# The shifted copies of the VectorE score groups are made on GpSimd, with 16 VectorE tiles per block

## The chip, the cores and the metric

The kernel runs on one core of a Trainium2 chip. The metric is the device time of one execution in microseconds (us). Three runs of the kernel before took 776.45, 778.93 and 774.36 us; the median is 776.45.

The core has five engines that run side by side, each in the order of its own list of instructions: PE (TensorE, matrix products), ACT (ScalarE, exponentials), DVE (VectorE), POOL (GpSimd) and SP (SyncE, which here issues nearly all DMAs). They wait for each other through semaphores.

## The reference

Two attentions share one input and are mixed by a gate. S is 2048, D is 512, there are 32 heads of 16.

```python
# A: linear attention with softmax features
phi_q = concat([softmax(pq), softmax(-pq)]);  phi_k = concat([softmax(pk), softmax(-pk)])
kv = einsum("bhsf,bhsd->bhfd", phi_k, v);  z = einsum("bhsf->bhf", phi_k)
o_A = einsum("bhqf,bhfd->bhqd", phi_q, kv) / (einsum("bhqf,bhf->bhq", phi_q, z)[..., None] + 1e-6)
# B: full attention
p = softmax(einsum("bhqd,bhkd->bhqk", q, k) * 16 ** -0.5)
o_B = einsum("bhqk,bhkd->bhqd", p, v)
g = sigmoid((x * gate_w).sum(-1))
out = g * (o_A @ A_wo) + (1 - g) * (o_B @ B_wo)
```

Nearly all the work lies in B: 32 heads of 2048 x 2048 scores, each of which needs an exponential.

## The kernel before

**Blocks and tiles.** B is cut into 32 blocks. A block is four heads and 512 queries; it has 16 tiles of 128 keys for each head, so 64 tiles of 128 x 512 scores, and 2048 tiles in all. The scores of a tile come from PE (`qk_mm`, line 782), land in PSUM and are made into exponentials in bf16. PE then multiplies them by the values (`pv_mm`, line 883) and adds them up in PSUM (psO); a column of ones in the values gives the sum of each softmax.

**Two ways to an exponential.** Most tiles go through ACT: `add_exp` (line 859) takes three tiles and two tiles by turns in one instruction (line 862), from one half of the six banks of psS. Those instructions are the slots by which the rest of the order is counted. The list DN (line 31) says how many tiles of each block take the other way, through DVE. There a tile is made in an integer: DVE reads the scores, adds a constant, clamps at zero and writes an int16 (line 840), whose bits, read as bf16, are a rough exponential. To make it better, the kernel uses three such values for each score, the number itself (t) and the number plus 35 (s) and plus 83 (m) (STEPS, line 28), and PE adds up all three: three matmuls a tile (`add_pvd`, line 886) where a tile of ACT needs one.

**Groups.** DVE's tiles are handled in groups of up to four (`add_group`, line 827). The scores of each tile go to a free bank (psM or the last bank of psS) by a matmul of their own; four evictions (line 840) fill a buffer t of 128 x 2048. Then two additions (line 853) write the buffers s and m. They are DVE instructions on int16 in SBUF. The buffers are taken in turn from rings of three or four (t), three (s) and three or two (m), mostly memory that other steps don't need at that time, which is why one line shows many tile names (Tx, Ty, vA, WAT, WoA and so on). A group can reuse a buffer once PE has read the old one. A field `pool` of each group is set from the list PN (line 56) at line 710; nothing in the kernel before reads it.

**Other work.** A's features are made 128 rows at a time in `phi` (line 1098): PE, two exponentials on ACT (line 1105), a sum of pairs on POOL (line 1110), a row sum and reciprocal on DVE (1112, 1114) and two products on POOL (line 1118). 16 such steps make phiK, one per 13 slots from slot 40, and 16 make phiQ, one per 14 slots from slot 270. For each pair of blocks, POOL also multiplies the result by its reciprocal sums (T2, line 983). The projections, A's second half and the output fill PE and DVE between the tiles. SP moves q, phiQ, the sums and the output.

**Order.** Nothing runs in the order in which the program names it. Each operation is given to a planner (`Plan`) with an engine, an estimated duration and a priority; `layout` (line 149) plays the execution through with these estimates and writes one fixed list for each engine. `emit` then puts a semaphore wait wherever an operation needs another engine's result. A group's operations carry priorities some 22 slots (D_AHEAD) ahead of the slot where its tiles are due. Operations marked `lock` on DVE (the additions, line 853, and one product per late block, line 998) and on POOL are laid apart in time: a locked POOL operation also waits for the last locked DVE operation ahead of it (lines 311 to 314). PE gets matmuls by zero (`zero_mm`, line 871) where the plan would leave it idle; they add nothing to the result.

Of the kernel before, what the change touches and what calls it, by code (L numbers as in the profile page):

```python
# [11 lines left out]
ALU = mybir.AluOpType  # L12
# [13 lines left out]
QSCALE = 0.25 * LOG2E * 2.0 ** 7  # L26
EXPB = 127.0 * 2.0 ** 7 - 252.7
STEPS = (35, 83)
ESCALE = math.log(2.0) / 2.0 ** 7

DN = (0, 10, 14, 16, 14, 16, 14, 16, 14, 16, 14, 16, 14, 16, 14, 16, 14, 16, 14, 16, 14, 16, 14, 16, 14, 16, 14, 16, 14, 16, 14, 12)
G_EARLY = 13
W_AT = 18.0
D_FIRST = 12
# [18 lines left out]
TURN_PAD = 4.0  # L53
G_DEEP = 6
K_AT, K_PACE, Q_AT, Q_PACE = 45.0, 13.0, 275.0, 13.5
PN = (1, 2, 1, 2, 1, 2, 1, 2, 1, 2, 1, 2, 1, 2, 1, 2, 1, 2, 1, 2, 1, 2, 1, 2, 1, 2, 1, 2, 1, 2, 1, 2)
D_AHEAD = 22.0
CONT = -60.0
EPAIRS = 5
# [326 lines left out]
def bass_gated_mix__linear_kernel_hedgehog__mha_block__prompt_kernel(  # L386
    nc: bass.Bass,
    A_x: bass.AP,
    A_wqkv: bass.AP,
    A_w_phi: bass.AP,  # L390
    A_wo: bass.AP,
    B_x: bass.AP,
    B_wqkv: bass.AP,
    B_wo: bass.AP,
    gate_w: bass.AP,
    out: bass.AP,
):
    with contextlib.ExitStack() as ctx:
        _build(ctx, nc, A_x, A_wqkv, A_w_phi, A_wo, B_wqkv, B_wo, gate_w, out)


def _build(ctx, nc, A_x, A_wqkv, A_w_phi, A_wo, B_wqkv, B_wo, gate_w, out):
# [71 lines left out]
    P = Plan()  # L474
# [20 lines left out]
    for rr in range(8):  # L495
# [4 lines left out]
                  name="woa", lat=5.0),  # L500
              dma("sp", 2.2, lambda e: e.dma_start(WoB[:], B_wo.rearrange("(t p) c -> p t c", p=128)), ["WoB"],
                  name="wob", lat=5.0)]
# [3 lines left out]
    def warm_fn(e):  # L506
        ins = None
        for _ in range(6):
# [5 lines left out]
    pool = lambda dur, prio, fn, reads=(), writes=(), name="": P.add("pool", dur, prio, fn, reads=reads,  # L514
                                                                    writes=writes, name=name)
# [3 lines left out]
         writes=["ident"], name="ident")  # L519
# [9 lines left out]
          writes=["pmask0"], name="pm0")  # L529
    P.add("dve", 0.1, -9, lambda e: e.tensor_scalar(pmask[:, 1:2], pmask[:, 0:1], -QSCALE, QSCALE, op0=ALU.mult,  # L530
                                                    op1=ALU.add), reads=["pmask0"], writes=["pmask1"], name="pm1")
    P.add("dve", 0.1, -9, lambda e: e.tensor_single_scalar(pmask[:, 0:1], pmask[:, 0:1], QSCALE, ALU.mult),
          reads=["pmask1"], writes=["pmask", "pmask0"], name="pm2")
# [6 lines left out]
    for t in range(KT):  # L540
# [12 lines left out]
          writes=["mtmp1"], name="mk0")  # L553
    P.add("dve", 0.12, 30, lambda e: e.tensor_single_scalar(mask64[:], m1, 16, ALU.is_lt), reads=["mtmp1"],
          writes=["mask64"], name="mk1")
    pool(0.3, -2, lambda e: e.tensor_copy(mask4[:], mask64[:].rearrange("p (j c) -> p j c", c=16)[:, :, 0]),
         reads=["mask64"], writes=["mask4"])
# [3 lines left out]
    def fill(prio, mms, reads, banks=None, name="", chunk=1, dur=MM, after=(), cols=NQ):  # L561

        f = Fill(MISC if banks is None else banks)
        prev = None
        for i in range(0, len(mms), chunk):
            part = mms[i:i + chunk]

            def fn(e, part=part):
                ins = None
                for m in part:  # L570
                    ins = m(e, f.ap())
                return ins
            op = P.add("pe", dur * len(part), prio if prev is None else CONT, fn, reads=reads if prev is None else (),
                       after=after if prev is None else [prev], name=f"{name}.{i}")
            op.full, op.fill = cols / 2400.0 * len(part), True
            if prev is None:
                op.acq = f
            prev = op
        for k in reads:
            P.readers.setdefault(k, []).append(prev)  # L580
        return f, prev

    def drain(f, mm, eng, dur, prio, fn, reads=(), writes=(), name="", last=True, after=()):
        op = P.add(eng, dur, min(prio, -20.0) if eng == "dve" else prio, lambda e: fn(e, f.ap()), reads=reads, writes=writes, after=[mm] + list(after),
                   name=name)
        if last:
            op.rel = f
        return op
# [109 lines left out]
    slots = []  # L698
    assert all(n % 2 == 0 for n in DN)
    dcount = [[0] * 4 for _ in range(NB)]  # L700
    dtiles, groups, turn = [], [], 0
    for b in range(NB):
        for k in range(DN[b]):
            i = (k + turn) % 4
            dcount[b][i] += 1
            dtiles.append(dict(t=(b, i, NT - dcount[b][i]), k=k))
        turn += DN[b]
        mine = dtiles[len(dtiles) - DN[b]:]
        for n in range(0, DN[b], 4):
            groups.append(dict(ts=mine[n:n + 4], left=len(mine[n:n + 4]), pool=n // 4 < PN[b] and len(mine[n:n + 4]) == 4))  # L710
    cur, rot = 0, 0

    def next_tile():
# [49 lines left out]
    def opening(name):  # L763
        if name in opened:
            return []
        opened.add(name)
        return list(bufs[name][1])

    def quarter(ap, q):
        if len(ap.shape) == 3:  # L770
            return ap[:, q // 2, 512 * (q % 2):512 * (q % 2) + 512]
        return ap[:, 512 * q:512 * q + 512]
# [7 lines left out]
    def qk_mm(e, t, bank):  # L780
        b, i, kt = t
        return e.matmul(bank, lhsT=kT_B[32 * i:32 * i + 32, b // 8 % 2, 128 * kt:128 * (kt + 1)],  # L782
                        rhs=qz[32 * i:32 * i + 32, b // 2 % 4, b % 2, :], start=True, stop=True,
                        tile_position=(32 * i, 0))
# [30 lines left out]
    def make_groups(n):  # L815
        for g in groups[made[0]:n]:
            if any(k in holder and holder[k]["left"] for k in (g["t"], g["s"], g["m"])):
                break
            holder[g["t"]] = holder[g["s"]] = holder[g["m"]] = g
            add_group(g)  # L820
            made[0] += 1

    def d_prio(d):
        b = d["t"][0]
        return first_slot[b] + d["k"] * 20.0 / DN[b] - D_AHEAD

    def add_group(g):
        t, s, m = (bufs[g[k]][0] for k in "tsm")
        ft, ops, tb = opening(g["t"]), [], t
        before = list(dq_ops)  # L830
        dq_ops.clear()
        for q, d in enumerate(g["ts"]):
            b, i, kt = d["t"]
            f, mm = fill(DQ_PRIO + DQ_K * d_prio(d), [lambda e, ap, t=d["t"]: qk_mm(e, t, ap)],
                         [kkey(b // 8, kt), ("q", b // 2 % 4, b % 2)], name=f"dq{b}.{kt}.{i}", dur=0.25,
                         after=[exp_ops[D_FIRST]] + ft + P.writer.get((g["t"], q), []) +
                         P.readers.get((g["t"], q), []) + before, cols=NQ)
            dq_ops.append(mm)
            mm.kind, mm.heads = "dq", [i]
            ops.append(drain(f, mm, "dve", 0.70, d_prio(d), lambda e, ap, q=q: e.tensor_scalar(  # L840
                quarter(tb, q).bitcast(I16), ap, EXPB, 0.0, op0=ALU.add, op1=ALU.max),
                writes=[(g["t"], q)], after=ft, name=f"D1.{b}.{kt}.{i}"))

        def add(dur, fn, reads, writes, name, after=()):
            ops.append(P.add("dve", dur, d_prio(g["ts"][0]) - 5.0, fn, reads=reads, writes=writes, after=after,
                             name=f"{name}.{b}.{kt}"))
            ops[-1].lock = True
        size = len(g["ts"])
        part = lambda ap: ap[:, 0:512 * size].bitcast(I16)
        t, s, m = part(t), part(s), part(m)  # L850
        tk = [(g["t"], k) for k in range(size)]
        for key, dst, step in (("s", s, STEPS[0]), ("m", m, STEPS[1])):
            add(0.72 if size == 4 else 0.45, lambda e, dst=dst, step=step: e.tensor_single_scalar(dst, t, step, ALU.add),  # L853
                tk, [g[key]], "D2" if key == "s" else "D3", opening(g[key]))
        if g is groups[-1]:
            last_d1.extend(ops[:size])
        phase_ops[g["ph"]].extend(ops)

    def add_exp(j):
        n = len(slots[j])  # L860
        base = 3 * (j % 2)
        op = P.add("act", 0.051 + 0.4267 * n, 0.0, lambda e: e.activation(  # L862
            Ebuf[:, j // 2 % EPAIRS, 1536 * (j % 2):1536 * (j % 2) + 512 * n], psS[:, 512 * base:512 * (base + n)], ACTF.Exp, scale=ESCALE),
            reads=[("S", j % 2)], writes=[("E", j % ERING)], name=f"exp{j}")
# [336 lines left out]
    for i in range(4):  # L1201
        mms = [lambda e, ap, i=i, t=t: e.transpose(ap.bitcast(BF16)[:, 128 * t:128 * (t + 1)],
                                                   xs[:, i, 128 * t:128 * (t + 1)], ident[:]) for t in range(KT)]
        f, mm = fill(-1.0, mms, [("xs", i), "ident"], FIRST, name=f"X{i}", chunk=4, dur=0.08, cols=128)
        x_mms.append(mm)
        dst = xT[:, :, 128 * i:128 * (i + 1)]
# [142 lines left out]
```

## Time and profile before

| | before |
|---|---|
| runs | 776.45, 778.93, 774.36 us (median 776.45) |
| span of the profiled execution, first to last instruction | 774.6 us |
| its own time | the profile gives the span alone |
| mean granted clock of TensorE | 0.991 |
| busy: PE, ACT, DVE, POOL | 718.3, 757.2, 585.0, 137.0 us |
| exponentials of three tiles, of two tiles (line 862) | 318, 319 |
| evictions of DVE tiles (line 840) | 456, median 0.68 us |
| additions (line 853) | 212 of 2048 elements, 32 of 1024; 160.9 us busy |
| POOL instructions | 32 at line 1110, 64 at line 1118, 15 at line 983, 30 at the start |

How to read it: busy time is the time in which an engine has at least one instruction under way. ACT's records overlap, since an instruction starts before the one ahead of it has ended; so the distance from start to start, not the length of a record, is what one instruction costs. A row of the groups gives line, engine and operation, output and input, partitions x elements and type, the count, then busy us and mean ns of one, then the idle time ahead of the group and what ended it. A row of the waits reads "who waited <- for whom: us in total, times, longest". "PEld" is PE's weight load, with which each matmul starts.

### The profile page before, as it was taken

The numbers are of one execution on the slowest core, as the hardware profiler recorded it, in microseconds if no ns is written. First come the engines' busy times: TensorE is split into PE (matmuls) and PEld (weight loads), VectorE is DVE, ScalarE is ACT, GpSimd is POOL, SyncE is SP. The second block draws the span as 40 slices with busy tenths as digits, with TensorE's granted clock in tenths as the row PEclk, the third lists the DMA queues.
The fourth block names the chain that finished last, engine by engine and source line by source line (L and its number), as shares of the span: only waits on it lengthen the run. The fifth ranks groups of instructions, "written<-read, shape, count | busy, mean of one in ns | idle before, by whom it ended". The sixth has DMA issues, their size and how long they took to land.

```text
span 774.6 us, 17058 instructions
## 1 busy us (share of the span) xinstructions
PE 718.3 (93%) x7135; PEld 223.1 (29%) x7194; DVE 585.0 (76%) x1023; ACT 757.2 (98%) x708; POOL 137.0 (18%) x141
## 2 busy tenths in 40 slices
PE   8999989998999999989999999998999998999999
PEld 4332222332322222332322222222232222222222
DVE  3667877777778888567898897987887778787842
ACT  6999999999999999999999999999999999999996
POOL 6001032112322131200313121231311200000000
PEclk9999999999999999998999999999999999999999
DMA  6600000000000100201002221322311221020101
GB/s 128 146 9 16 20 14 21 10 23 9 10 17 9 24 8 8 72 8 23 23 27 60 55 71 44 82 68 51 83 53 38 73 53 37 22 64 3 46 13 48
DMA packets 67933, 30.72 MB, mean 40 GB/s; under 512 B 53208, under 2 KB 62808, under 8 KB 67856
## 3 DMA queue, kind: packets, MB, share of 16 engines
q1 hardware_dynamic: 66368, 28.95, 14.9%
q8 instruction: 56, 0.92, 0.5%
q10 hardware_dynamic: 1104, 0.66, 0.3%
q0 software_dynamic: 384, 0.02, 0.1%
q14 instruction: 21, 0.17, 0.1%
HBM read 7.87 MB, written 8.88 MB: 22 GB/s over the span
## 4 chain that ended last, share of the span: by engine, by line
ACT 84%; PE 11%; DVE 4%; SPq 1%; DMA 1%; issue 1%
ACT E_t L862 80%; ACT EA_t L1105 3%; PE psS L782 3%; PE psO L883 3%; PE psM L591 1%; PE psS L591 1%; DVE Tx_t L840 1%; DVE WAT_t L840 1%; PE psO L873 1%; DMA xT_t<-in_A_x_dram 1%; SPq L486 0%; DVE vA_t L853 0%; PE psS L651 0%; DVE vA_t L840 0%; DVE Ty_t L853 0%
## 5 line engine op out<-in xcount | busy, mean ns | idle before, releaser
L862 ACT ACTIVATE E_t<-psS 128x1536 bf16<-128x1536 f32 x637 | 731.9, 1419 | 5.4 <-PE psS L782 3.7
L782 PE MATMUL psS<-qz_t,kTB_t 32*128 32x512 bf16 x1815 | 277.0, 387 | 41.9 <-ACT E_t L862 34.1
L782 PEld LDWEIGHTS psS<-qz_t,kTB_t 32*128 32x128 bf16 x1815 | 69.2, 91 | 277.8 <-ACT E_t L862 242.3
L883 PE MATMUL psO<-E_t,vaug_t 128*32 128x512 bf16 (+1 forms) x1592 | 141.1, 389 | 0.7 <-DVE vaug_t L647 0.5
L840 DVE TENSOR_SCALAR Tx_t<-psS 128x512 int16<-128x512 f32 x121 | 82.4, 681 | 27.2 <-PE psS L782 24.6
L840 DVE TENSOR_SCALAR Tx_t<-psM 128x512 int16<-128x512 f32 x127 | 86.8, 683 | 19.4 <-PE psM L782 17.7
L873 PE MATMUL psO<-xT_t,zero_t 128*32 128x512 bf16 x1076 | 93.8, 387 | 0.0
L1110 POOL TENSOR_TENSOR half_t<-EA_t 128x512 f32<-128x512 bf16 x32 | 37.0, 1155 | 314.0 <-ACT EA_t L1105 273.4
L782 PE MATMUL psM<-qz_t,kTB_t 32*128 32x512 bf16 x233 | 90.1, 387 | 0.7 <-DVE Tx_t L840 0.2
L883 PE MATMUL psO<-vA_t,vaug_t 128*32 128x512 bf16 (+1 forms) x430 | 58.7, 387 | 0.0
L883 PE MATMUL psO<-Ty_t,vaug_t 128*32 128x512 bf16 (+1 forms) x308 | 50.4, 390 | 0.0
L1118 POOL TENSOR_TENSOR phiQ_t<-EA_t,stat_t 128x512 bf16<-128x512 bf16 x32 | 34.2, 1070 | 72.2 <-DVE stat_t L1114 61.7
L983 POOL TENSOR_TENSOR oT_t<-Tf_t,Rb_t 128x512 bf16<-128x512 f32 x15 | 19.1, 1272 | 157.4 <-DVE Ty_t L853 91.1
L883 PEld LDWEIGHTS psO<-E_t,vaug_t 128*32 128x32 bf16 (+1 forms) x1592 | 29.0, 95 | 59.8 <-issue 57.1
L1118 POOL TENSOR_TENSOR phiK_t<-EA_t,stat_t 128x512 bf16<-128x512 bf16 x32 | 33.8, 1058 | 60.4 <-DVE stat_t L1114 31.3
L883 PE MATMUL psO<-Tx_t,vaug_t 128*32 128x512 bf16 (+1 forms) x248 | 38.5, 398 | 0.0
L873 PEld LDWEIGHTS psO<-xT_t,zero_t 128*32 128x32 bf16 x1076 | 23.3, 94 | 41.3 <-issue 36.2
L853 DVE TENSOR_SCALAR vA_t<-Tx_t 128x2048 int16<-128x2048 int16 x50 | 34.1, 686 | 0.1
L853 DVE TENSOR_SCALAR Ty_t<-Tx_t 128x2048 int16<-128x2048 int16 x42 | 29.8, 709 | 0.4
L840 DVE TENSOR_SCALAR WAT_t<-psM 128x512 int16<-128x512 f32 x37 | 25.2, 682 | 5.9 <-PE psM L782 3.8
L840 DVE TENSOR_SCALAR WAT_t<-psS 128x512 int16<-128x512 f32 x39 | 26.6, 682 | 2.2 <-PE psS L782 1.9
L782 PEld LDWEIGHTS psM<-qz_t,kTB_t 32*128 32x128 bf16 x233 | 21.1, 91 | 23.1 <-issue 6.7
(188 smaller groups left out, 768.1 us busy)
## 6 DMA issues: line engine op xcount, KB each, us to landing
dpq<-phiQ_t SPq DMA_DIRECT2D x16, 256.0 KB, 2.1
Rb_t<-lr SPq DMA_DIRECT2D x120, 32.0 KB, 1.8
dpo<-oA_t SPq DMA_DIRECT2D x16, 128.0 KB, 1.8
qz_t<-qz_t SPq DMA_DIRECT2D x120, 16.0 KB, 1.8
Tf_t<-Tf_t SPq DMA_DIRECT2D x60, 32.0 KB, 2.0
out_dram<-WvA_t SPq DMA_DIRECT2D x14, 128.0 KB, 1.7
WB_t<-in_B_wqkv_dram SPq DMA_DIRECT2D x3, 384.0 KB, 4.4
WvA_t<-in_A_wqkv_dram SPq DMA_DIRECT2D x1, 512.0 KB, 4.0
```

Source lines behind the costliest of these rows:

```text
L591: return [lambda e, ap, i=i: e.matmul(ap, lhsT=lhs[i], rhs=rhs[i], start=(i == 0), stop=(i == len(lhs) - 1)) for i in range(len(lhs))]
L782: return e.matmul(bank, lhsT=kT_B[32 * i:32 * i + 32, b // 8 % 2, 128 * kt:128 * (kt + 1)], rhs=qz[32 * i:32 * i + 32, b // 2 % 4, b % 2, ...
L840: ops.append(drain(f, mm, "dve", 0.70, d_prio(d), lambda e, ap, q=q: e.tensor_scalar(quarter(tb, q).bitcast(I16), ap, EXPB, 0.0, op0=ALU.a ...
L853: add(0.72 if size == 4 else 0.45, lambda e, dst=dst, step=step: e.tensor_single_scalar(dst, t, step, ALU.add), tk, [g[key]], "D2" if key ...
L862: op = P.add("act", 0.051 + 0.4267 * n, 0.0, lambda e: e.activation(Ebuf[:, j // 2 % EPAIRS, 1536 * (j % 2):1536 * (j % 2) + 512 * n], psS ...
L873: ins = e.matmul((psO if bank is None else bank)[32 * i:32 * i + 32, :], lhsT=zero[:], rhs=xT[:, 0, 0:NQ], start=bank is not None, stop=ba ...
L883: return e.matmul(psO[32 * i:32 * i + w, :], lhsT=vaug[:, kt, o:o + w], rhs=rhs, start=start, stop=stop, tile_position=(0, 32 * i), skip_g ...
L983: P.add("pool", 1.1, -40, lambda e: e.tensor_tensor(oT[:, r, qc, :], Tf[:, 0, :], Rb[:], ALU.mult), reads=[("Tf", 0), "Rb"], writes=[("oT" ...
L1105: ins = e.activation(EA[:, b, :].rearrange("p (g s c) -> p s g c", s=2, c=64)[:, sgn, :, :], ap.rearrange("p (g c) -> p g c", c=64), ACTF. ...
L1110: P.add("pool", 1.15, prio, lambda e: e.tensor_tensor(half[:], e3[:, :, 0:8], e3[:, :, 8:16], ALU.add), reads=[("EA", b)], writes=["half"] ...
L1118: parts.append(P.add("pool", 1.0, prio, lambda e, n=n: e.tensor_tensor(dst[:, 512 * n:512 * n + 512].rearrange("p (g f) -> p g f", f=DH), ...
```

## The change

The two additions of every group go from DVE to POOL. There each is one `tensor_scalar` with two operations, times 1.0 and plus 35 or 83. The planner is told 0.2 us plus 512 x tiles / 1200 us for it (1.9 us for four tiles), it has the same priority as before, and it is marked `lock`. PN is 4 for all blocks, and the condition that a group has four tiles is gone, so all groups take this way. With no additions on DVE, its only locked operation left is the product of the last blocks. DN becomes 16 for all blocks but the first three and the last, where 14 and 16 took turns: DVE tiles go from 456 to 484, tiles of ACT from 1592 to 1564.

```diff
+G_FIX = 0.2
-DN = (0, 10, 14, 16, 14, 16, 14, 16, 14, 16, 14, 16, 14, 16, 14, 16, 14, 16, 14, 16, 14, 16, 14, 16, 14, 16, 14, 16, 14, 16, 14, 12)
+DN = (0, 10, 14) + (16,) * 28 + (12,)
-PN = (1, 2, 1, 2, 1, 2, 1, 2, 1, 2, 1, 2, 1, 2, 1, 2, 1, 2, 1, 2, 1, 2, 1, 2, 1, 2, 1, 2, 1, 2, 1, 2)
+PN = (4,) * 32
-            groups.append(dict(ts=mine[n:n + 4], left=len(mine[n:n + 4]), pool=n // 4 < PN[b] and len(mine[n:n + 4]) == 4))
+            groups.append(dict(ts=mine[n:n + 4], left=len(mine[n:n + 4]), pool=n // 4 < PN[b]))
         for key, dst, step in (("s", s, STEPS[0]), ("m", m, STEPS[1])):
+            if g["pool"]:
+                ops.append(P.add("pool", G_FIX + 512 * size / 1200.0, d_prio(g["ts"][0]) - 5.0, lambda e, dst=dst, step=step: e.tensor_scalar(
+                    dst, t, 1.0, float(step), op0=ALU.mult, op1=ALU.add), reads=tk, writes=[g[key]],
+                    after=opening(g[key]), name=f"G{key}.{b}.{kt}"))
+                ops[-1].lock = True
+                continue
             add(0.72 if size == 4 else 0.45, lambda e, dst=dst, step=step: e.tensor_single_scalar(dst, t, step, ALU.add),
```

## The prediction

> **What bounds the kernel now.** I read the busy times first, then the chain that ended last, then who waited for whom.
>
> ```profile
> PE 718.3 (93%) x7135; PEld 223.1 (29%) x7194; DVE 585.0 (76%) x1023; ACT 757.2 (98%) x708; POOL 137.0 (18%) x141
> ...
> ACT 84%; PE 11%; DVE 4%; SPq 1%; DMA 1%; issue 1%
> ```
>
> ACT is busy 757.2 of 774.6 us and carries 84% of the chain. PE is nearly as busy, so the waits must say which of the two waits for the other:
>
> ```profile
> PEld psS L782 <- ACT E_t L862: 242.3, 543, 1.2
> ```
>
> 543 times PE's weight loads for the next scores stood still until an exponential had freed its PSUM banks. PE follows ACT. The chain in order of time gives the price of one exponential where nothing disturbs it:
>
> ```profile
> 602.77 63.29 ACT E_t L862 x56
> ```
>
> 63.29 / 56 = 1.130 us per exponential; they alternate between three and two tiles, so one tile costs ACT 1.130 / 2.5 = 0.452 us. DVE (76%) and POOL (18%) have room. So a tile taken from ACT is worth 0.452 us, as long as DVE, POOL and PE keep up; time taken from DVE alone is worth nothing.
>
> **Part 1, tiles moved from ACT to VectorE.** DN sums to 456 before (10 + 15 x 14 + 14 x 16 + 12) and 484 after (10 + 14 + 28 x 16 + 12). 28 tiles leave ACT: 28 x 0.452 = 12.7 us. As a cross-check, 1592 tiles were 637 exponentials; 1564 are 626, and 11 x 1.130 = 12.4 us. I take 12.7.
>
> **Part 2, what the 28 tiles add.** On DVE: 28 evictions of 0.68 us (L840) = 19 us. On PE, 28 scores matmuls run by themselves instead of inside ACT's slots, and 84 term matmuls replace 28: line 883 has 2962 records in 249 us busy, 0.084 us each, so 56 x 0.084 = 4.7 us, and at most 28 x 0.33 us (the spacing of single scores matmuls around 603 us) = 9 us; some 10 to 14 us in all. PE's filler matmuls (L873) take 100 us and are laid only where PE has nothing else. That cover hides it; where there is none (666 to 683 us, where the chain runs on PE) it could cost up to its share, under 1 us.
>
> **Part 3, what leaves DVE.** 244 additions (L853), 160.9 us busy. They lie beside ACT, so I price them at nothing. One side effect is visible. Two stretches of the timeline, DVE, then POOL:
>
> ```profile
> 106.82 0.68 DVE L840 TENSOR_SCALAR Tx_t<-psM 128x512 int16<-128x512 f32 x1
> 107.42 1.16 DVE L853 TENSOR_SCALAR WoA_t<-Tx_t 128x2048 int16<-128x2048 int16 x1
> ```
>
> ```profile
> 106.98 1.06 POOL L1118 TENSOR_TENSOR phiK_t<-EA_t,stat_t 128x512 bf16<-128x512 bf16 x1 [0.63 <-DVE Ty_t L853]
> ```
>
> An addition beside a GpSimd operation took 1.16 us instead of 0.68 (up to 1.52 elsewhere), and GpSimd waited for one before it started. An eviction from PSUM beside the same operation kept 0.68; none of the 456 evictions exceeds 0.693. So additions and GpSimd exclude each other, evictions and GpSimd don't: after the change POOL can run all the time without slowing DVE. DVE falls to about 585 - 161 + 19 = 443 us (57%). GpSimd's order no longer waits for DVE's last addition, which also shortens the phi chains.
>
> **Part 4, what POOL gets.** 122 groups, 120 of four tiles and two of two: 240 additions of 2048 elements and 4 of 1024. All depends on the duration d of one. No row shows it. The nearest:
>
> ```profile
> L1118 POOL TENSOR_TENSOR phiQ_t<-EA_t,stat_t 128x512 bf16<-128x512 bf16 x32 | 34.2, 1070 | 72.2 <-DVE stat_t L1114 61.7 <-DVE vA_t L853 9.8
> ...
> L538 POOL MEMSET qz_t<- 128x1536 bf16 x1 | 1.4, 1378 | 0.0
> ...
> L518 POOL TENSOR_SCALAR ident_t<-ident_t 128x128 bf16<-128x128 bf16 x1 | 0.5, 547 | 0.0
> ...
> L523 POOL TENSOR_SCALAR mtmp_t<-ptmp_t 128x32 f32<-128x32 f32 x1 | 0.3, 283 | 0.0
> L526 POOL TENSOR_TENSOR ptmp_t<-mtmp_t 128x32 f32<-128x32 f32 x1 | 0.3, 254 | 0.0
> ...
> L535 POOL MEMSET zero_t<- 128x32 bf16 x1 | 0.1, 125 | 0.1
> ```
>
> Each kind has a short and a long row, so each has a slope:
> - Memset, nothing read: (1378 - 125) / (1536 - 32) = 0.83 ns an element; 2048 elements: 0.125 + 2016 x 0.00083 = **1.8 us**, the lower end.
> - Two tensors read: (1057 - 254) / 480 = 1.67 ns (1057 is the usual one); 0.254 + 2016 x 0.00167 = **3.6 us**.
> - The same operation as the new one (TENSOR_SCALAR), but comparing: (547 - 283) / 96 = 2.75 ns; **5.8 us**, the upper end. The long row is a single one and in the kernel's first two microseconds, and a comparison isn't a sum, so I trust its slope least.
>
> The addition reads one tensor where L1118 reads two: half its slope gives 0.254 + 2016 x 0.00084 = 1.94 us. Two L1118 back to back took 2.19 us from the first start to the last end, so 1.13 from start to start, 0.07 above the record. I take **d = 2.0 us**, near memset and half of L1118, and keep 1.8 and 5.8 for the range. The diff's planner cost, 0.2 + 2048 / 1200 = 1.9 us, says only for which d the order is laid out.
>
> The Trainium skill speaks against the move: "GPSIMD Engine Reference", section 4.1, gives elementwise work on a tile to VectorE, though it calls one-input work on GpSimd roughly line-rate. Its section 3.1 has a best loop of 1.8 cycles an element at 1.2 GHz: 2048 of them would be an estimated 3.1 us, with which the sum below would give about 926 us. By line rate the sum is the one I take; no row of this trace decides between the page's two statements.
>
> **Part 5, has POOL room for it?** The share over the whole span (18%) misleads, as POOL's phi work is bunched. The timeline cut by stage (columns: PE, PEld, DVE, ACT, POOL busy, clock, DMA, GB/s):
>
> ```profile
> 50.00:300.00 250.00, 233.24 (x2313) 71.53 (x2333) 198.77 (x327) 250.00 (x240) 53.17 (x48) 1.00 0.06 14
> 300.00:350.00 50.00, 44.92 (x475) 15.41 (x474) 33.36 (x58) 49.97 (x46) 6.57 (x6) 0.99 0.13 35
> 350.00:575.00 225.00, 209.26 (x2106) 63.11 (x2122) 188.92 (x342) 223.40 (x214) 52.29 (x47) 0.99 0.20 54
> 575.00:775.00 200.00, 186.76 (x1812) 54.42 (x1821) 138.43 (x249) 190.74 (x172) 11.62 (x10) 0.98 0.15 40
> ```
>
> By the same cut line 840 has 160, 28, 149 and 110 evictions in these stages. Times 484 / 456, and two additions for four evictions: 84.9, 14.9, 79.1 and 58.4 additions. The stages shrink by 12.7 us in all, to 246, 49, 221 and (to 751 us, the last addition) 173 us. POOL needs:
> - 50 to 300: 84.9 d + 53.2, full at d = 2.27; at 2.0 it is 223 of 246 us (91%)
> - 350 to 575: 79.1 d + 52.3, full at d = 2.14; at 2.0 it is 210 of 221 us (95%)
> - the other two are full at 2.8 to 2.9.
>
> So d decides, and the turn is close above my value. Beyond it, each 0.1 us costs (84.9 + 79.1) x 0.1 = 16 us.
>
> **The wait that is added.** PE's term matmuls for 35 and 83 now wait for POOL, and POOL takes 2 d = 4.0 us for a group where DVE took about 1.2. Groups are started some 22 slots (25 us) ahead, which covers that. Behind a waiting addition on POOL stand the phi sums (L1110), on which DVE's row sums wait, and T2 (L983). Behind a waiting term on PE stand the next scores, then ACT; a block's last PV needs all its terms. At 95% full some additions will come late; I put 2.5 us for it, an estimate between none and the whole gain of 12.7. No DMA moves: qz, phi and output transfers stay on SP and are issued only somewhat earlier or later.
>
> **Sum.** Span 774.6 - 12.7 + 2.5 = 764.4 us. The profile gives the span and no separate total for its execution; the median of the runs, 776.45, is 1.9 us above the span, and I keep that: 764.4 + 1.9 = **766.3 us**.
>
> **Rivals.**
> - A, forecast: POOL keeps up (d of 1.8 to 2.1), ACT stays the bound: 766.3, between 755 and 772. The lower end adds what ACT loses inside its records, 731.9 - 637 x 1.130 = 12 us, most of which the move can't touch. For it: the memset and two-tensor slopes, evictions undisturbed by GpSimd. Chance 0.56.
> - B, the other side: POOL becomes the bound between 50 and 575 us; ACT gets gaps and waits for PE, PE for POOL. It decides from d = 2.2 on. With A's 763.7 (no lateness) as base: d = 2.3 gives 2.5 + 12.8 more, 779; d = 2.6 gives 828; d = 3.6 some 1050 (all four stages over); d = 5.8 some 1570. For it: the TENSOR_SCALAR rows. Against: they compare. Chance 0.31, of which 0.12 below 815.
> - C, no difference: d is near 2.15, or additions come late at block ends, and the gain goes as PE waiting for terms and ACT for PE: 773 to 780. For it: 95% of POOL between 350 and 575 us. Against: 25 us of lead. Chance 0.13.
>
> A measurement of this kernel tells about 0.5% (3.9 us) from no change. Faster by more: 0.57 (A and the edge of C); within: 0.12; slower: 0.31. The range runs from 755 to 815; above it lies 0.19, all B.
>
> **What would show it.** Part 1: 626 exponentials at 1.13 us. Part 3: DVE near 57%, no additions left. Part 4: 244 POOL operations at the new line, back to back at 2.0 us; POOL near 137 + 240 x 2.0 + 2 = 619 us (81%). Part 5: POOL nearly full from 350 to 575 us, ACT still near 98%. I am wrong if the additions take over 2.2 us, or if ACT shows gaps behind PE's terms.

## The result and the profile after

The changed kernel takes 768.63 us (median of four runs, 767.56 to 770.39) against 777.27 us for the kernel before: a ratio of 0.9892, 95% interval 0.9864 to 0.9920. Run again later, beside the last experiments (e10_again), it took 766.75 us, ratio 0.9876 (0.9849 to 0.9902). The forecast was 766.3 us, within 755 to 815.

The page after, busy times and the chain:

```profile
PE 712.5 (93%) x7121; PEld 220.9 (29%) x7174; DVE 473.2 (62%) x807; ACT 744.7 (97%) x697; POOL 594.5 (78%) x385
...
ACT 86%; PE 8%; POOL 2%; DVE 1%; issue 1%; SPq 1%; DMA 1%; POOLq 0%
...
L869 ACT ACTIVATE E_t<-psS 128x1536 bf16<-128x1536 f32 x626 | 719.6, 1429 | 7.9 <-PE psS L783 5.5
```

Lines have moved down: exponentials are line 869, evictions 841, term matmuls 890, the additions on GpSimd 855. ACT still carries the chain. There are 626 exponentials, busy 719.6 us against 731.9 for 637 before. POOL is at 594.5 us, DVE at 473.2 (62%; forecast were 619 and 443 us). The span went from 774.6 to 765.5 us: 12.5 us less of ACT's busy time (757.2 to 744.7), 3.4 us more of ACT idle (17.4 to 20.8). Now POOL, one addition after another (start, us, operation):

```profile
399.11 1.90 POOL L855 TENSOR_SCALAR vA_t<-WAT_t 128x2048 int16<-128x2048 int16 x1
401.09 1.90 POOL L855 TENSOR_SCALAR Ty_t<-vA_t 128x2048 int16<-128x2048 int16 x1
403.06 1.90 POOL L855 TENSOR_SCALAR vA_t<-vA_t 128x2048 int16<-128x2048 int16 x1
```

An addition lasts 1.90 us and costs 1.98 from start to start. The two phi stages, to be read beside those of before (columns PE, PEld, DVE, ACT, POOL, clock, DMA, GB/s):

```profile
50.00:300.00 250.00, 235.32 (x2325) 71.55 (x2343) 160.31 (x258) 249.25 (x239) 212.32 (x133) 0.99 0.06 14
...
350.00:575.00 225.00, 209.24 (x2132) 61.97 (x2142) 145.61 (x259) 221.94 (x213) 196.36 (x124) 0.98 0.21 52
```

POOL went from 53 to 212 us and from 52 to 196 us, 85% and 87% by its records. ACT stood idle for 0.75 us in the first and 3.1 us in the second; before it was none and 1.6.

The largest new gap lies between 530 and 540 us. Three views of it: pieces of the chain, ACT's own order, and busy times with the granted clock in the third column from the right.

```profile
526.16 1.86 POOL Ty_t L855
528.03 0.08 issue
528.11 1.90 POOL vA_t L855
...
530.08 1.16 POOL half_t L1117
```

```profile
528.38 7.36 ACT L869 ACTIVATE E_t<-psS 128x1024 bf16<-128x1024 f32 x6
536.21 1.02 ACT L869 ACTIVATE E_t<-psS 128x1024 bf16<-128x1024 f32 x1 [0.47 <-PE psS L783]
538.58 1.45 ACT L869 ACTIVATE E_t<-psS 128x1536 bf16<-128x1536 f32 x1 [1.34 <-PE psM L783]
```

```profile
528.00:536.00 8.00, 6.41 (x62) 1.83 (x59) 5.49 (x15) 7.60 (x8) 6.98 (x6) 0.82 0.13 38
536.00:544.00 8.00, 8.00 (x83) 2.00 (x80) 4.28 (x7) 6.32 (x6) 5.00 (x4) 0.76 0.39 104
```

The chain goes over POOL, whose operations follow each other without a pause. Then PE, busy 6.41 of 8 us, is granted half its clock for some 7 us (0.82 and 0.76 are the means of the two stretches), and ACT waits for PE. The gap of before had the same look, with no POOL in it:

```profile
350.00:360.00 10.00, 9.84 (x82) 2.82 (x81) 6.48 (x11) 8.57 (x8) 0.00 (x0) 0.69 0.08 14
```

So part of ACT's idle time goes with clock dips that occur in both kernels. Between 50 and 750 us ACT stood idle for 3.6 us before and 4.9 after. Cut into stretches of ten us, 3.4 us of the first and 3.5 of the second lie in stretches with a dip; at full clock there was next to none before, and some 1.1 us after (0.1 near 320 us, and 1.0 between 440 and 460 us, where POOL's additions are on the chain). Over 17 runs of the kernel before, 0.001 more mean clock went with 0.40 us less time. The two kernels' means are 0.988 to 0.992 and 0.991, so dips explain little of the difference between them.

### The profile page after: what moved, and what is told of

Its sections match the earlier page's. It is cut to its first block, busy times and chain, and to the rows that moved or that the text cites. A ratio compares the mean times of both kernels' runs of the same rounds, so it can differ in the third digit from the quotient of the medians.

```text
span 765.5 us, 17004 instructions
## 1 busy us (share of the span) xinstructions
PE 712.5 (93%) x7121; PEld 220.9 (29%) x7174; DVE 473.2 (62%) x807; ACT 744.7 (97%) x697; POOL 594.5 (78%) x385
## 4 chain that ended last, share of the span: by engine, by line
ACT 86%; PE 8%; POOL 2%; DVE 1%; issue 1%; SPq 1%; DMA 1%; POOLq 0%
ACT E_t L869 82%; ACT EA_t L1112 4%; PE psO L890 2%; PE psS L783 2%; PE psS L592 2%; POOL vA_t L855 1%; PE psM L592 1%; DMA xT_t<-in_A_x_dram 1%; SPq L487 0%; POOL half_t L1117 0%; DVE vA_t L841 0%; POOL Ty_t L855 0%; DVE Tf_t L974 0%; PE psM L783 0%; PE psS L880 0%
## 5 line engine op out<-in xcount | busy, mean ns | idle before, releaser
L869 ACT ACTIVATE E_t<-psS 128x1536 bf16<-128x1536 f32 x626 | 719.6, 1429 | 7.9 <-PE psS L783 5.5
L890 PE MATMUL psO<-E_t,vaug_t 128*32 128x512 bf16 x1564 | 137.5, 388 | 0.5 <-DVE vaug_t L648 0.5
L855 POOL TENSOR_SCALAR vA_t<-Tx_t 128x2048 int16<-128x2048 int16 x50 | 95.2, 1904 | 11.9 <-DVE Tx_t L841 4.5
L855 POOL TENSOR_SCALAR Ty_t<-Tx_t 128x2048 int16<-128x2048 int16 x42 | 79.7, 1898 | 27.2 <-DVE Tx_t L841 25.3
L855 POOL TENSOR_SCALAR vA_t<-WAT_t 128x2048 int16<-128x2048 int16 x26 | 49.3, 1898 | 17.1 <-PE psO L890 12.5
L890 PE MATMUL psO<-vA_t,vaug_t 128*32 128x512 bf16 x472 | 57.9, 387 | 1.6 <-POOL vA_t L855 1.3
L855 POOL TENSOR_SCALAR vA_t<-vA_t 128x2048 int16<-128x2048 int16 x24 | 45.5, 1898 | 7.5 <-PE psO L890 5.8
L1117 POOL TENSOR_TENSOR half_t<-EA_t 128x512 f32<-128x512 bf16 x32 | 37.0, 1155 | 16.2 <-ACT EA_t L1112 14.4
L890 PEld LDWEIGHTS psO<-E_t,vaug_t 128*32 128x32 bf16 x1564 | 28.0, 95 | 56.6 <-issue 53.9
L1119 DVE TENSOR_REDUCE stat_t<-half_t 128x64 f32<-128x512 f32 x32 | 21.8, 680 | 24.6 <-POOL half_t L1117 24.5
L890 PE MATMUL psO<-Tx_t,vaug_t 128*32 128x512 bf16 x248 | 36.5, 390 | 0.0
L841 DVE TENSOR_SCALAR vA_t<-psS 128x512 int16<-128x512 f32 x37 | 25.5, 688 | 14.8 <-PE psS L783 14.3
```

Source lines behind the costliest of these rows:

```text
L855: ops.append(P.add("pool", G_FIX + 512 * size / 1200.0, d_prio(g["ts"][0]) - 5.0, lambda e, dst=dst, step=step: e.tensor_scalar(dst, t, 1. ...
L890: return e.matmul(psO[32 * i:32 * i + w, :], lhsT=vaug[:, kt, o:o + w], rhs=rhs, start=start, stop=stop, tile_position=(0, 32 * i), skip_g ...
L1117: P.add("pool", 1.15, prio, lambda e: e.tensor_tensor(half[:], e3[:, :, 0:8], e3[:, :, 8:16], ALU.add), reads=[("EA", b)], writes=["half"] ...
L1119: P.add("dve", 0.66, prio, lambda e: e.tensor_reduce(stat[:, b, 1, :], half[:], AX.X, ALU.add), reads=["half"], writes=[("ss", b)], name=f ...
```

## The experiments

Ratios are to the kernel before on the same chip; intervals are 95%.

| run | us | ratio (interval) | clock |
|---|---|---|---|
| e1_move_only | 774.98 | 0.9968 (0.9951 to 0.9985) | 0.999 |
| e2_tiles_only | 773.17 | 0.9949 (0.9929 to 0.9969) | 0.988 |
| e3_one_op | 1536.58 | one run | 0.70 |
| e4_pool_1024 | 799.24 | 1.0285 (1.0260 to 1.0310) | 0.986 |
| e4_pool_512 | 772.75 | 0.9945 (0.9923 to 0.9968) | 0.983 |
| e5_dn18 | 805.71 | 1.0367 (1.0340 to 1.0394) | 0.981 |
| e6_pn3 | 766.60 | 0.9874 (0.9850 to 0.9897) | 0.992 |
| e7_forms | 1356.12 | one run | 0.73 |
| e8_truth | 764.51 | 0.9843 (0.9817 to 0.9869) | 0.992 |
| e9_pn3_all | 768.55 | 0.9889 (0.9864 to 0.9913) | 0.986 |
| e9_pn2_all | 764.52 | 0.9843 (0.9815 to 0.9871) | 0.992 |
| e10_again | 766.75 | 0.9876 (0.9849 to 0.9902) | 0.992 |

The clock is the mean over the runs, the only value where there is one run.

### The move alone

```diff
-DN = (0, 10, 14) + (16,) * 28 + (12,)
+DN = (0, 10, 14, 16, 14, 16, ..., 14, 16, 14, 12)   # as before
```

> The additions go to GpSimd, but DN stays as before (456 VectorE tiles). Theory: ACT sets the pace, DVE's time is worth nothing, so the time stays within 0.5% of the kernel before (773 to 781 us), with 637 exponentials. Rival: the additions on DVE held up the order (they and GpSimd exclude each other), so the move alone brings a good part of the 8.6 us, 772 us or less. Second rival: the longer additions on GpSimd come late at block ends, and without the 28 tiles the kernel is slower than before, 781 us or more.

It took 774.98 us, 0.3% under the kernel before, in the band of the first theory.

```profile
PE 725.2 (94%) x7354; PEld 223.6 (29%) x7410; DVE 458.4 (59%) x779; ACT 756.4 (98%) x708; POOL 571.1 (74%) x385
```

Its twelve runs have a mean clock of 0.999 where the runs of before have 0.991; by the slope of 0.40 us per 0.001, that is some 3.3 us, more than the 2.7 gained. The two of the twelve with a clock like that of before (0.993 and 0.991) took 777.56 and 779.39 us, and none of the runs of before at these clocks took more than 778.3. So at the same clock, moving 161 us of work off DVE shows no gain by itself. Whether the move is what raises the clock in this run is open: more of PE's filler matmuls (1376 against 1160) would fit, but that was not tested. In the changed kernel the clock is not raised.

### The tiles alone

```diff
-PN = (4,) * 32
+PN = (0,) * 32
```

> DN is 16 as in the changed kernel (484 VectorE tiles, 626 exponentials), but all additions stay on DVE. If the 28 tiles are the whole gain and DVE has room for them, the time is that of the changed kernel, 766 to 770 us, and GpSimd was not needed. If DVE is what limited the number of tiles (busy 84% between 350 and 575 us before, some 90% with the tiles, and held up by GpSimd's phi work), the groups come late and the time is 774 us or more, with gaps on ACT behind PE's terms.

773.17 us lies between the two cases. ACT has its 626 exponentials, as in the changed kernel, but the gain is 4.5 us, where the changed kernel gained 8.6. DVE is at 187.7 of 225 us between 350 and 575 us (83%), not 90%.

```profile
PE 717.7 (93%) x7027; PEld 225.8 (29%) x7086; DVE 603.8 (78%) x1051; ACT 745.5 (97%) x697; POOL 137.2 (18%) x141
```

```profile
ACT WvA_t L1060 <- PE psM L592: 7.0, 1, 7.0
```

In the profiled run ACT is idle 770.3 - 745.5 = 24.8 us, 4 more than in the changed kernel at the same clock (0.989). Some 2 of these 4 us lie in one wait at the very end, for a projection of PE (7.0 us, in the changed kernel 4.9); the rest is in small pieces, and the chain goes through PE (14%) and DVE (4%) in many small pieces too, so why the order is later I can't name.

With the 28 tiles in place, then, moving the additions is worth something: 0.9892 (0.9864 to 0.9920) with the move and 0.9949 (0.9929 to 0.9969) without it don't overlap. Neither part alone gives the whole gain. That the two need each other is argued and not shown: as raw times the gains of the two parts add up to 2.7 + 4.5 = 7.2 us, which the intervals (about 1.3, 1.6 and 2.2 us) don't separate from 8.6. It rests on taking the 2.7 us for a matter of the clock.

### One operation or two

```diff
-                    dst, t, 1.0, float(step), op0=ALU.mult, op1=ALU.add), reads=tk, writes=[g[key]],
+                    dst, t, float(step), ALU.add), reads=tk, writes=[g[key]],   # e.tensor_single_scalar
```

> The changed kernel, but each addition on GpSimd is one single-operation instruction (plus the shift) in place of times one, plus the shift. If only the element count matters (one input, d near the slope of memset), d stays 1.9 us and the time 768 us. If the single operation is as slow as the two rows of TENSOR_SCALAR at the start of the kernel (2.75 ns an element), d is some 5.8 us, POOL is the bound and the time is some 1570 us by the stage sum of the prediction.

1536.58 us, twice the time. POOL's row, and who waits:

```profile
L855 POOL TENSOR_SCALAR vA_t<-Tx_t 128x2048 int16<-128x2048 int16 x50 | 268.2, 5366 | 9.0 <-DVE Tx_t L841 3.5 <-PE psM L1138 1.8
```

```profile
ACT E_t L869 <- PE psS L783: 566.8, 181, 17.7
...
PEld psO L890 <- POOL vA_t L855: 197.1, 56, 6.0
```

The same sum on the same buffers takes 5.37 us instead of 1.90. The waits now run the other way round: PE's terms wait for POOL, and ACT for PE. The two short TENSOR_SCALAR rows of the kernel before, 2.75 ns an element, came near it: the rows of 2048 and 1024 elements here (5366 and 2770 ns) give 2.54 ns.

### Which two operations

```diff
+FORMS = (lambda x: (1.0, x, ALU.mult, ALU.add), lambda x: (x, 1.0, ALU.add, ALU.mult),
+         lambda x: (x, 0.0, ALU.add, ALU.add), lambda x: (x, 0.0, ALU.add, ALU.max))
-                    dst, t, 1.0, float(step), op0=ALU.mult, op1=ALU.add), ...
+                    dst, t, c[0], c[1], op0=c[2], op1=c[3]), ...   # c: form of the group's number modulo 4
```

> The changed kernel with four forms of the two-operation instruction by turns over the groups: times one then plus; plus then times one; plus then plus zero; plus then the maximum with zero (same numbers). If any two operations avoid the 5.4 us of the single one, all four forms take 1.9 us and the time is 768 us. If only times-then-plus is fast, three of four groups take 5 us or more and the time is some 1300 us. The records of the four forms tell them apart.

```profile
397.15 7.08 POOL L857 TENSOR_SCALAR phiQT_t<-oT_t 128x2048 int16<-128x2048 int16 x1
404.31 7.08 POOL L857 TENSOR_SCALAR oT_t<-oT_t 128x2048 int16<-128x2048 int16 x1
411.46 1.90 POOL L857 TENSOR_SCALAR Ty_t<-Tx_t 128x2048 int16<-128x2048 int16 x1
413.44 1.90 POOL L857 TENSOR_SCALAR WoA_t<-Tx_t 128x2048 int16<-128x2048 int16 x1
```

In the early blocks the buffer tells the form, since the ring of t has four and the forms go by fours: Tx holds the first two forms, phiQ the third, oT the fourth. All sums from Tx into WoA, WoB, phiQT and oT, which only these blocks have, take 1.90 us; those from phiQ and oT 7.08. So a product and a sum, in either order, is fast; two sums, or a sum and a maximum, are slower than one sum alone. Neither the number of operations nor that of inputs decides, but the pair. Both cases of the expectation are refuted: not every pair is fast, and times-then-plus is not the only fast one. That 1356 us lies near the 1300 of the second case is luck, since two forms of four are slow, not three, and each takes 7.1 us, not 5.

### More work on POOL

```diff
+            ops.append(P.add("pool", G_FIX + 1024 / 1200.0, ..., lambda e: e.tensor_scalar(
+                s[:, 0:1024], t[:, 0:1024], 1.0, float(STEPS[0]), op0=ALU.mult, op1=ALU.add), reads=tk, writes=[g["s"]], ...))   # 512 for 1024 in e4_pool_512
-        for key, dst, step in (("s", s, STEPS[0]), ("m", m, STEPS[1])):
+        for key, dst, step in (("m", m, STEPS[1]), ("s", s, STEPS[0])):
```

> The changed kernel with one more addition of 1024 elements on GpSimd per group (it writes half of s, which the full addition then writes again; m is made before s). With additions of 1.98 us from start to start and some 1.0 us for the extra one, the mean cost is as if d were 2.47 us. Theory (stage sum: 84.9 d + 53.2 against 246 us, 79.1 d + 52.3 against 221 us): POOL is over by 17 us and 26 us in the two phi stages, and the time is 800 to 815 us. Rival: POOL has buffers and lead enough, ACT stays the bound: under 775 us. Second rival: lateness weighs more than the sum, as every group is late by a microsecond at each block end: over 825 us.

> As the run with an extra addition of 1024 elements per group, but of 512 elements (some 0.6 us): as if d were 2.27 us. The stage sum turns at 2.27 between 50 and 300 us and at 2.14 between 350 and 575 us: POOL is over by some 10 us in the second stage alone, and the time is 774 to 784 us. If the turn is sharper or comes later than the sum has it (the run with 1024 elements was 8 us under the sum), 769 to 773 us. If any lateness on POOL reaches ACT, over 785 us.

The extra instruction takes 1.05 us (1.12 from start to start) or 0.62 (0.70), so the mean addition costs (2 x 1.98 + 1.12) / 2 = 2.54 us or 2.33 us. The times are 799.2 us, just under the 800 to 815 expected, and 772.8, which is the case of a later turn. With 1024 elements:

```profile
PE 736.7 (92%) x7367; PEld 231.5 (29%) x7426; DVE 468.8 (59%) x807; ACT 748.1 (94%) x697; POOL 717.9 (90%) x507
...
ACT 42%; POOL 37%; PE 15%; issue 3%; DVE 2%; SPq 1%; DMA 1%; POOLq 0%
```

```profile
ACT E_t L874 <- PE psO L895: 23.4, 13, 7.0
```

POOL carries nearly as much of the chain as ACT: rival B, made to happen, with ACT waiting behind PE's terms. But it begins later than the prediction's stage sum has it. By stages, d = 2.33 would give 763.7 + 5 + 15 = 784 us and d = 2.54 some 818; measured were 773 and 799. Taking the four stages as one, 237.3 d + 123.7 against 689 us, gives nothing over at 2.33 and 37 us over at 2.54, so 764 and 801. That fits much better at 2.54 (2 us off in place of 19), and hardly better at 2.33 (9 us under, in place of 11 over). The stages of the run with 1024 elements:

```profile
50.00:300.00 250.00, 235.74 (x2332) 72.72 (x2353) 154.99 (x249) 248.11 (x238) 237.86 (x164) 1.00 0.06 14
...
350.00:575.00 225.00, 205.93 (x2096) 62.66 (x2110) 138.59 (x248) 209.94 (x199) 218.57 (x149) 0.98 0.16 42
```

In the first stage POOL is nearly full, with 237.9 of 250 us in records; yet ACT stands idle there for 1.9 us alone, where the stage sum has 23. The changed kernel had 133 instructions on POOL in that stage, 86 of them additions; 43 extra ones would make 176, and there are 164, so about a dozen came later. ACT's idle time comes later: 15.1 us between 350 and 575 us and 14.4 between 575 and 775. So POOL does carry work over the edge of a stage; how far the lead of 22 slots is what allows it was not tested.

### Eighteen tiles

```diff
-DN = (0, 10, 14) + (16,) * 28 + (12,)
+DN = (0, 10, 14) + (18,) * 28 + (12,)
```

> The changed kernel with 18 VectorE tiles per block in place of 16; the fifth group, of two tiles, keeps its additions on DVE. 56 more tiles leave ACT, worth up to 56 x 0.452 = 25 us. If ACT is still what bounds, and PE's fillers and DVE's room cover the rest, 745 to 758 us. If POOL (98% between 350 and 575 us with the shorter blocks) or PE take over, the time stays at 762 us or more.

805.71 us. ACT has 603 exponentials, but waits 58 us in all ahead of them. One gap is special:

```profile
377.37 3.28 ACT L869 ACTIVATE E_t<-psS 128x1024 bf16<-128x1024 f32 x3 [20.77 <-PE psO L890]
```

On the chain, where the gap begins, stand a matmul of line 1138, which reads A's values, and then two additions into their memory, which the late blocks use as buffers. They are the first of nine additions that POOL makes without a pause from 357.9 to 375.9 us, and the gap ends at 377.4. This looks like a backlog that waited for that memory, but was not tested. Without this gap the kernel would still be near 785 us by subtraction, with PE busy 95% and on 28% of the chain. POOL is not full (188 of 225 us between 350 and 575 us). So 18 tiles in this order are too many; what limits them, PE, this buffer or the fifth group's additions, which are back on DVE, was not separated, and 17 was not tried.

### Some additions back to DVE

```diff
-PN = (4,) * 32
+PN = (4,) * 14 + (3,) * 10 + (4,) * 8   # e6_pn3;  (3,) * 32 in e9_pn3_all;  (2,) * 32 in e9_pn2_all
```

> The changed kernel, but in blocks 14 to 23 (about 350 to 575 us) one group of four keeps its additions on DVE, so that POOL falls from some 90% to 75% there. If POOL's lateness between 350 and 575 us is what cost the changed kernel the difference between 12.7 and 8.6 us, the time falls to 763 to 766 us. If the missing microseconds lie elsewhere (PE's clock, PE-bound pieces), or if additions on DVE and GpSimd's work hold each other up again, it stays at 767 us or rises.

> The changed kernel with three groups of each block on GpSimd and the fourth on DVE (three quarters of the additions moved). If lateness on POOL in the phi stages is the loss that is left, 765 to 767 us, as where only blocks 14 to 23 had three. If a few additions on DVE already bring the hold-ups between DVE and GpSimd back, 769 us or more.

> The changed kernel with two groups of each block on GpSimd (half of the additions moved). Between none moved (773.2 us) and all moved (768.6): if DVE's room is what counts and half of it is enough, 765 to 769 us; if the hold-ups grow with the additions that share the time with GpSimd's, 770 us or more.

> The changed kernel once more, on the chip of the three runs above: 767 to 770 us. It gives the base that these runs are compared with.

766.6, 768.6 and 764.5 us, against 768.6 and 766.8 for all on GpSimd and 773.2 for none. The first and the second each fall between their two cases and don't decide between them; the third lies just under its first case, that half is enough. On one chip the last three runs, with three quarters, half and all of the additions on GpSimd, have overlapping intervals (0.9889, 0.9843 and 0.9876). What holds: half of the additions on GpSimd (POOL 372 us, DVE 547) is as good as all of them. That three quarters come out above a half is not explained; its mean clock is 0.006 lower, some 2.4 us by the slope above.

### The planner told the truth

```diff
-                ops.append(P.add("pool", G_FIX + 512 * size / 1200.0, ...
+                ops.append(P.add("pool", 0.27 + 512 * size / 1200.0, ...   # and 1.1 for 1.0 (phi), 1.25 for 1.1 (T2)
```

> The changed kernel, but the planner is told POOL's durations as measured from start to start: 0.27 + 512 x tiles / 1200 us for an addition (1.98 for four tiles, before 1.91), 1.1 for the phi products (1.0) and 1.25 for T2 (1.1). If the planner's optimism is what made POOL late, the time falls by 1 to 3 us. If the order is as good as it gets with all additions on POOL, it stays within 1 us of the changed kernel, 767 to 770 us.

764.51 us, ratio 0.9843 (0.9817 to 0.9869), 2.2 us under the changed kernel on the same chip, where that has 0.9876 (0.9849 to 0.9902). The intervals overlap, so a gain over the changed kernel is likely but not certain; over the kernel before it is 1.6%. Between 350 and 575 us ACT now has no idle time:

```profile
350.00:575.00 225.00, 214.21 (x2184) 63.03 (x2184) 146.75 (x261) 225.00 (x216) 199.17 (x125) 1.00 0.20 52
```

POOL is as busy there as in the changed kernel (199 and 196 us). Two things differ in this profile. The 1.0 us of ACT's idle time between 440 and 460 us, at full clock behind POOL's additions, is gone. And no clock dip falls into this stage, where the profile of e10_again has one near 536 us with 1.4 us of idle time beside it; here the dips fall at 580 and 605 us, with 2.0 us. So about 1 us is what the true lengths can be seen to give. This and half of the additions on DVE are the fastest versions found.

## Why the prediction was right

**The bound.** Rival A came true, at 768.63 and 766.75 us: ACT was and stays the bound. The move alone gave 2.7 us, and nothing at the same clock, as "time taken from DVE alone is worth nothing" had it. But DVE's time is not free in company: without the move the tiles bring only 4.5 us. The prediction did not ask whether DVE could have taken the tiles with the additions; this was missing.

**The 28 tiles.** 12.7 us forecast; ACT's busy time fell by 12.5.

**DVE.** The forecast of 443 us (57%) was 30 us too low: measured were 473.2. The sum took the records of the additions as if each stood alone. Records of DVE overlap (the addition at 107.42 us starts before the eviction ahead of it ends, at 107.50), so the run that moved the additions alone lost 126.7 us of busy time, not 160.9. It had no bearing on the time.

**POOL's addition.** d was taken as 2.0 us and is 1.98 from start to start. The number was right, in part by luck, since its reason holds only half. "The addition reads one tensor where L1118 reads two: half its slope" is refuted as a rule: the single addition also reads one tensor and takes 5.37 us. The rows that I trusted least, TENSOR_SCALAR at 2.75 ns, give what one operation costs. Memset's 0.83 ns is what a product with a sum costs: (1897 - 1044) / 1024 = 0.83 ns. That this memset was the right row to take was not known either: the same trace has one of 128 x 512 that took 2.29 us (line 536, which writes with gaps), and the prediction doesn't weigh it. That the change writes its sum as such a pair is worth 768 us in a total of 1537. Rival B at 31% was no formality: its upper end, some 1570 us at 5.8, was the other form of the same sum. The Trainium skill's "GPSIMD Engine Reference", section 4.1, calls one-input work on GpSimd roughly line-rate. Taking memset's 0.83 ns an element for that rate, the product with a sum reaches it here (0.83 ns), and none of the three other forms does (2.54 ns for one sum, 7.08 us in place of 1.90 for the other two).

**POOL's room and the lateness.** Forecast were 91% and 95% in the two phi stages. The records show 85% and 87%, to which 0.08 us between two additions has to be added, some 3%. The 2.5 us for late additions stand against 3.4 us more of ACT's idle time, but not all of that is lateness: 1.3 us of it lie between 50 and 750 us, where some 1.1 us follow POOL at full clock, and the rest before 50 us, beside a clock dip, and at the end. So the size of this term came out near, and its content only in part. With POOL's true durations in the plan, a profile shows no idle ACT in the second phi stage, but no clock dip there either.

**The turn.** "Decides from d = 2.2 on" was too early, and the stage sum too steep near the turn: at 2.33 the kernel is still faster than before (0.9945), and at 2.54 it is 19 us under the sum. The step that failed here is that each stage was held to be full by itself: in the run with 1024 elements, POOL carried about a dozen instructions out of the first phi stage, and ACT hardly noticed there. At the changed kernel's d of 1.98 this did not matter.

**The exclusion.** Part 3 takes GpSimd's wait for an addition as a sign that the two exclude each other. That wait shows only the order that the program lays (a locked POOL operation waits for the last locked DVE operation); what the trace shows is the other half, additions of up to 1.52 us in place of 0.68 beside GpSimd's work.

**Evictions beside GpSimd.** They did stay whole: none above 0.694 us with POOL at work for 78% of the span. The median of most groups rose from 0.681 to 0.691, but not through GpSimd: in the kernel before, evictions that start after a pause of DVE take 0.690 us on average, the 49 beside GpSimd's work like the 83 others, and those that follow another instruction directly 0.67 to 0.68. After the change 269 of 484 follow a pause, before 132 of 456.

## What to carry to other kernels

Before moving elementwise work to GpSimd, time the very form of the instruction there: the same sum cost 1.9, 5.4 or 7.1 us depending on what stood beside it. Price what an engine is freed of by what can be put in its place on the engine that bounds, and try both parts separately, since here neither alone gave the gain. In a planned order, tell the planner the durations as measured from start to start: here, corrections of 4 to 14% on POOL came with 2.2 us less, as much as moving half of the additions back, though neither is certain against the changed kernel.

## What the runs showed of the hardware that was not expected

- GpSimd, TENSOR_SCALAR on int16, 128 x 2048: product and sum in either order 1.90 us; one sum 5.37; two sums, or a sum and a maximum, 7.08. Per element, from the rows of 1024 and 2048: 0.83, 2.54 and, for two sums, about 3.4 ns.
- DVE's evictions from PSUM take 0.690 us after a pause of DVE and 0.67 to 0.68 behind another instruction, whether GpSimd works beside them or not.
- TensorE's clock falls to half for stretches of 3.4 to 10.2 us, at varying places, in the profiles of before, of the changed kernel and of the first two experiments. With POOL as the bound and PE waiting for it, its mean was 0.70 and 0.73.
